# Two-layer decode attention with feed-forward: streaming K and weights past narrow operands in four column groups

## Chip, cores and metric

One core of one Trainium2 chip. The metric is the device time of the program in microseconds (us). Runs are given as a median with the lowest and highest in brackets. The ratio of two kernels is the mean time of the one's fast runs over that of the other's of the same rounds, so it is not quite the ratio of the medians quoted. The profile of a run covers one execution; its span is some 2 us shorter than the run time.

## The reference, cut to what matters

```python
# B=4 batches, 1 token each, D=512, 32 query heads, 8 K/V heads, 4096 keys, head size 128, F=1792; bf16
def A(x, k_cache, v_cache, wq, wo):
    q = (x @ wq) ...                                   # per head
    scores = einsum("bhqd,bhkd->bhqk", q, k) * Dh**-0.5
    o = einsum("bhqk,bhkd->bhqd", softmax(scores), v)
    return o.reshape(B, 1, Hq*Dh) @ wo
def Bf(x, w_gate, w_up, w_down):
    return (gelu(x @ w_gate) * (x @ w_up)) @ w_down
x = A_x
x = x + A(layernorm(x), ...);  x = x + Bf(layernorm(x), ...)
x = x + A(layernorm(x), ...);  x = x + Bf(layernorm(x), ...)   # same caches and weights again
```

Both layers read the same K and V caches. The kernel keeps the turned K of one batch on chip, so K crosses once and V twice: 114.6 MB in all. The pipeline runs over batches: attention of layer 1 for batch 0, then a **dense part** (projection, feed-forward, second-layer queries), then a **two-layer stage** (second-layer scores and softmax of batch b beside K, scores and V of the first layer of batch b+1), and so on. The dense parts of batches 1 to 3 run beside the second-layer V tiles of the batch before. A last attention and a last feed-forward over all four batches end it.

## The kernel before

K is loaded in tiles of 128x2048 bf16 (512 KB) and turned in 32x32 blocks by VectorE. A score matmul then loads 128x128 of turned K as weights and passes 16 columns of a padded query block through it. Projections and feed-forward work the same way: 128x128 of weights loaded for one column of activations.

```python
class Turner:                      # one K tile: VectorE turns it in two halves
    def step(self):
        kn = load_kv(A_k_cache, self.b, kvh, t, "k_t")          # one of 7 buffers, shared with V
        for bb in range(NB):
            nc.vector.transpose(out=self.kt[:, ..., bb], in_=kf[:, :, bb])        # 128x512 fp32

def scores_head(sc, s, kt, kvh, qb):                            # 32 pairs for a head
    for g in range(G8):
        for be in range(BE):
            nc.tensor.matmul(sc[:, s, g, :], lhsT=kt[:, g, be // 2, :, be % 2],
                             rhs=qb[:, kvh, be].rearrange("p a h -> p (a h)"), ...)

def soft_max(sc):                  # two heads at a time
    nc.vector.tensor_reduce(out=colmax[:], in_=v, axis=AX.X, op=ALU.max)
    nc.gpsimd.partition_all_reduce(gmax..., colmax..., P, RED.max)
# ... soft_exp: subtract (VectorE), exp (ScalarE); soft_sum: reduce (VectorE), all-reduce (GpSimd)

def ffn_in(b0, nb, w_sb, name):    # 56 pairs; out_proj, q_proj and down alike
    for m in range(KF):
        for k in range(KD):
            nc.tensor.matmul(h[:, m, :], lhsT=w_sb[:, k, m * P:(m + 1) * P], rhs=xn_bf[:, k, bs], ...)
```

Of the kernel before, what the change touches and what calls it, by code (L numbers as in the profile page):

```python
# [15 lines left out]
P = 128  # L16
# [3 lines left out]
CH = 16  # L20
GH = 2
QD = 4
# [3 lines left out]
KV_BUFS = 7  # L26
# [3 lines left out]
def kernel(  # L30
# [20 lines left out]
    assert Sq == 1 and Dh == P and rep == 4  # L51
# [3 lines left out]
    NT = C // CH  # L55
    NG = Hkv // GH
    G8 = C // QD
    HG = GH * rep
    assert C % CH == 0 and CH % QD == 0
# [5 lines left out]
    ktp = ctx.enter_context(tc.tile_pool(name="ktp", bufs=Hkv))  # L65
    kvin = ctx.enter_context(tc.tile_pool(name="kvin", bufs=KV_BUFS))
    qbp = ctx.enter_context(tc.tile_pool(name="qbp", bufs=2))
    rawp = ctx.enter_context(tc.tile_pool(name="rawp", bufs=2))
    p1p = ctx.enter_context(tc.tile_pool(name="p1p", bufs=2))
    p2p = ctx.enter_context(tc.tile_pool(name="p2p", bufs=NG))  # L70
    grp = ctx.enter_context(tc.tile_pool(name="grp", bufs=2))
    small = ctx.enter_context(tc.tile_pool(name="small", bufs=1))
# [3 lines left out]
    ps_acc = ctx.enter_context(tc.tile_pool(name="ps_acc", bufs=1, space=bass.MemoryType.PSUM))  # L76
    ps_misc = ctx.enter_context(tc.tile_pool(name="ps_misc", bufs=2, space=bass.MemoryType.PSUM))
# [3 lines left out]
    ident_bf = const.tile([P, P], BF16, name="ident_bf")  # L81
    make_identity(nc, ident_bf[:])
    mean_f = const.tile([P, P], FP32, name="mean_f")
    nc.vector.memset(mean_f[:], 1.0 / D)
    magic = const.tile([P, B], I32, name="magic")
    nc.vector.memset(magic[:], 0x5F3759DF)
    sel = const.tile([P, NB, 2, QD, QS], BF16, name="sel")
    for a in range(QD):
        nc.vector.tensor_copy(
            out=sel[:, :, :, a, :],  # L90
            in_=ident_bf[:].rearrange("p (b i e) -> p b e i", b=NB, e=2))
    amask = const.tile([P, QD], FP32, name="amask")
    nc.vector.tensor_reduce(out=amask[:], in_=ident_bf[:].rearrange("p (a i) -> p a i", a=QD),
                            axis=AX.X, op=ALU.max)
# [5 lines left out]
    wd_sb = wts.tile([P, KF, D], BF16, name="wd_sb")  # L100
    wq_dram = A_wq.rearrange("(k p) n -> p k n", p=P)
# [5 lines left out]
    q1_bf = state.tile([P, Hq, B], BF16, name="q1_bf")  # L107
    q2_bf = state.tile([P, Hq], BF16, name="q2_bf")
    xn_bf = state.tile([P, KD, B], BF16, name="xn_bf")

    dq = nc.sync
# [7 lines left out]


# [4 lines left out]
    def ln_center(b0, nb):  # L125
        bs = slice(b0, b0 + nb)
        st = ps_misc.tile([P, 2, nb, KD], FP32, name="st", tag="misc")
        nc.tensor.matmul(st[:], lhsT=mean_f[:, :], rhs=XX[:, :, bs], start=True, stop=True)  # L128
        mv = small.tile([P, 2, nb], FP32, name="mv", tag="mv")
        nc.vector.tensor_reduce(out=mv[:], in_=st[:], axis=AX.X, op=ALU.add)  # L130
        nc.vector.tensor_tensor(out=xn_bf[:, :, bs].rearrange("p k b -> p b k"), in0=XX[:, 0, bs],
                                in1=mv[:, 0].unsqueeze(2).broadcast_to([P, nb, KD]),
                                op=ALU.subtract)
        return mv
# [25 lines left out]
    def q_proj(b0, nb, h0, hp):  # L160
        bs = slice(b0, b0 + nb)
        qps = ps_misc.tile([P, hp, nb], FP32, name="qps", tag="misc")
        for i in range(hp):
            m = h0 + i
            for k in range(KD):
                nc.tensor.matmul(qps[:, i, :], lhsT=wq_sb[:, k, m * Dh:(m + 1) * Dh],  # L166
                                 rhs=xn_bf[:, k, bs], start=(k == 0), stop=(k == KD - 1))
        return qps

    def q_norm(qps, dst, rstd, hp, nb):  # L170
        nc.vector.tensor_tensor(out=dst, in0=qps[:], in1=spread_rstd(rstd, hp, nb), op=ALU.mult)  # L171

    def q_spread(q_rows, qb, h0, hp):
        k0, nk = h0 // rep, hp // rep
        qe = ps_misc.tile([P, nk, BE, rep], FP32, name="qe", tag="misc")
        for be in range(BE):
            nc.tensor.matmul(qe[:, :, be], lhsT=sel[:, be // 2, be % 2].rearrange("p a i -> p (a i)"),  # L177
                             rhs=q_rows, start=True, stop=True)
        nc.vector.tensor_tensor(  # L179
            out=qb[:, k0:k0 + nk].rearrange("p k n a h -> p (k n) a h"),  # L180
            in0=qe.rearrange("p k n h -> p (k n) h").unsqueeze(2)
                .broadcast_to([P, nk * BE, QD, rep]),
            in1=amask[:].unsqueeze(1).unsqueeze(3).broadcast_to([P, nk * BE, QD, rep]),
            op=ALU.mult)

    def out_proj(y, o_bf, h0, hp, first, last):
        for i in range(h0, h0 + hp):
            rhs = o_bf[:, i:i + 1] if len(o_bf.shape) == 2 else o_bf[:, i, :]
            for dk in range(KD):
                nc.tensor.matmul(y[:, :, dk], lhsT=wo_sb[:, i, dk * P:(dk + 1) * P], rhs=rhs,  # L190
                                 start=(first and i == h0 and dk == 0),
                                 stop=(last and i == h0 + hp - 1 and dk == KD - 1),
                                 skip_group_check=True)

    def add_y(b0, nb, y):
        bs = slice(b0, b0 + nb)
        nc.vector.tensor_tensor(out=XX[:, 0, bs], in0=XX[:, 0, bs], in1=y[:], op=ALU.add)  # L197

    def ffn_in(b0, nb, w_sb, name):
        bs = slice(b0, b0 + nb)  # L200
        h = ps_misc.tile([P, KF, nb], FP32, name=name, tag="misc")
        for m in range(KF):
            for k in range(KD):
                nc.tensor.matmul(h[:, m, :], lhsT=w_sb[:, k, m * P:(m + 1) * P],  # L204
                                 rhs=xn_bf[:, k, bs], start=(k == 0), stop=(k == KD - 1))
        return h

    def gelu(nb, hg, rstd):
        h = small.tile([P, KF, nb], FP32, name="h", tag="h")
        nc.vector.tensor_tensor(out=h[:], in0=hg[:], in1=spread_rstd(rstd, KF, nb), op=ALU.mult)  # L210
# [7 lines left out]
                                       in1=spread_rstd(rstd, KF, nb), op0=ALU.mult, op1=ALU.mult)  # L218
        nc.vector.scalar_tensor_tensor(out=sq[:], in0=sq[:], scalar=1.0, in1=h[:],
                                       op0=ALU.add, op1=ALU.mult)  # L220
        return sq

    def gate_up(nb, th, hu):
        H_bf = small.tile([P, KF, nb], BF16, name="H_bf", tag="H_bf")
        nc.vector.tensor_tensor(out=H_bf[:], in0=hu[:], in1=th[:], op=ALU.mult)
        return H_bf

    def down(nb, H_bf):
        y = ps_misc.tile([P, nb, KD], FP32, name="y2", tag="misc")
        for dk in range(KD):  # L230
            for k in range(KF):
                nc.tensor.matmul(y[:, :, dk], lhsT=wd_sb[:, k, dk * P:(dk + 1) * P],  # L232
                                 rhs=H_bf[:, k, :], start=(k == 0), stop=(k == KF - 1))
        return y


    KT = {}

    class Turner:
# [3 lines left out]
        def step(self):  # L243
            kvh, t = divmod(self.n, NT)
            self.n += 1
            if t == 0:
                self.kt = ktp.tile([P, G8, NB, QD, QS], FP32, name="kt", tag="kt")
                KT[kvh] = self.kt
            gt = CH // QD
            kn = load_kv(A_k_cache, self.b, kvh, t, "k_t")  # L250
            kf = kn.rearrange("p c d -> p (c d)").bitcast(FP32).rearrange(
                "p (c b i) -> p c b i", b=NB, i=QS)
            for bb in range(NB):
                nc.vector.transpose(  # L254
                    out=self.kt[:, t * gt:(t + 1) * gt, bb].rearrange("p g c j -> p g (c j)"),
                    in_=kf[:, :, bb])

    def new_scores():
        return ps_sc.tile([P, GH, G8, QD * rep], FP32, name="sc", tag="sc")

    def scores_head(sc, s, kt, kvh, qb):
        kt = kt.rearrange("p g b c j -> p (g b c j)").bitcast(BF16).rearrange(
            "p (g b m e) -> p g b m e", b=NB, m=P, e=2)
        for g in range(G8):
            for be in range(BE):
                nc.tensor.matmul(sc[:, s, g, :], lhsT=kt[:, g, be // 2, :, be % 2],  # L266
                                 rhs=qb[:, kvh, be].rearrange("p a h -> p (a h)"),
                                 start=(be == 0), stop=(be == BE - 1))

    def soft_max(sc):  # L270
        v = sc.rearrange("p s g (a h) -> p s h (g a)", h=rep)
        colmax = grp.tile([P, GH, rep], FP32, name="colmax", tag="col")
        nc.vector.tensor_reduce(out=colmax[:], in_=v, axis=AX.X, op=ALU.max)  # L273
        gmax = grp.tile([P, GH, rep], FP32, name="gmax", tag="all")
        nc.gpsimd.partition_all_reduce(gmax.rearrange("p s h -> p (s h)"),  # L275
                                       colmax.rearrange("p s h -> p (s h)"), P, RED.max)
        return gmax

    def soft_exp(sc, gmax):
# [277 lines left out]
```

## Time and profile before

| | |
|---|---|
| time | 368.95 us, median of 3 (367.92 to 370.53) |
| span of the profiled run | 373.3 us |
| traffic | 114.58 MB; a 512 KB tile takes 1.28 us at full rate |
| TensorE | 55% busy, 13,700 instructions of about 27 ns a pair |
| VectorE | 43% busy |

The profiled execution was a long one: a span of 373.3 us belongs to a run of some 375 us, 6 above the median. Its stage marks so lie up to that much late.

Two of the page's cost groups of the kernel before carry the change (columns: line, engine, operation, output and input, shapes, count, then busy us and mean ns of one, then the engine's idle time before it and what ended most of it):

```profile
L254 DVE STREAM_TRANSPOSE kt<-k_t 128x512 f32<-128x512 f32 x128 | 82.8, 686 | 26.9 <-DMA k_t<-in_A_k_cache_dram 16.8
L266 PE MATMUL sc<-qb,kt 128*128 128x16 bf16 x2048 | 63.0, 175 | 17.5 <-issue 13.6
```

The turn of K is VectorE's greatest item. The score matmuls are 2048 small ones. Their mean of 175 ns is a latency in a pipeline; the spacing is 27 ns.

### The profile page before, as it was taken

The numbers are of one execution on the slowest core, as the hardware profiler recorded it, in microseconds if no ns is written. First come the engines' busy times: TensorE is split into PE (matmuls) and PEld (weight loads), VectorE is DVE, ScalarE is ACT, GpSimd is POOL, SyncE is SP. The second block draws the span as 40 slices with busy tenths as digits, with TensorE's granted clock in tenths as the row PEclk, the third lists the DMA queues.
The fourth block names the chain that finished last, engine by engine and source line by source line (L and its number), as shares of the span: only waits on it lengthen the run. The fifth ranks groups of instructions, "written<-read, shape, count | busy, mean of one in ns | idle before, by whom it ended". The sixth has DMA issues, their size and how long they took to land.

```text
span 373.3 us, 14915 instructions
## 1 busy us (share of the span) xinstructions
PE 204.4 (55%) x6848; PEld 193.2 (52%) x6848; DVE 160.4 (43%) x502; ACT 26.5 (7%) x70; POOL 25.1 (7%) x70
## 2 busy tenths in 40 slices
PE   0435141337765545865555657656465557678645
PEld 0334141337665445764555647655465456677635
DVE  0854423303686553321777453127745523224104
ACT  0020000000011011000011010000101000001100
POOL 0000000000010111000111110000110100002000
DMA  7999999995078799999879899998888799984730
GB/s 237 421 417 383 416 375 417 395 407 228 11 253 302 234 376 363 382 313 359 288 244 386 347 329 377 358 341 275 271 332 308 265 382 413 345 311 147 248 119 2
DMA packets 36302, 115.52 MB, mean 309 GB/s; under 512 B 3208, under 2 KB 9104, under 8 KB 36240
## 3 DMA queue, kind: packets, MB, share of 16 engines
q1 hardware_dynamic: 36240, 114.58, 83.7%
q8 instruction: 53, 0.87, 0.9%
q14 instruction: 9, 0.07, 0.0%
HBM read 114.56 MB, written 0.00 MB: 307 GB/s over the span
## 4 chain that ended last, share of the span: by engine, by line
PE 38%; DMA 29%; issue 16%; DVE 15%; POOL 1%; ACT 1%; SPq 0%; ACTq 0%; POOLq 0%; DVEq 0%
DMA v_t<-in_A_v_cache_dram 29%; PE sc L266 11%; PE ot L334 10%; DVE kt L254 7%; PE qps L166 3%; PE y L190 3%; DVE colmax L273 2%; PE y L232 2%; PE hg L204 2%; PE hu L204 2%; PE x L293 1%; PE st L128 1%; DVE sc L281 1%; POOL gmax L275 1%; PE yf L190 1%
## 5 line engine op out<-in xcount | busy, mean ns | idle before, releaser
L334 PE MATMUL ot<-pe,v_t 128*128 128x4 bf16 x2048 | 68.7, 167 | 77.2 <-DMA v_t<-in_A_v_cache_dram 60.1
L334 PEld LDWEIGHTS <-v_t 128*128 128x128 bf16 x2048 | 63.7, 105 | 82.4 <-DMA v_t<-in_A_v_cache_dram 63.8
L254 DVE STREAM_TRANSPOSE kt<-k_t 128x512 f32<-128x512 f32 x128 | 82.8, 686 | 26.9 <-DMA k_t<-in_A_k_cache_dram 16.8
L266 PE MATMUL sc<-qb,kt 128*128 128x16 bf16 x2048 | 63.0, 175 | 17.5 <-issue 13.6
L266 PEld LDWEIGHTS <-kt 128*128 128x128 bf16 x2048 | 58.9, 104 | 20.0 <-issue 15.2
L273 DVE TENSOR_REDUCE colmax<-sc 128x8 f32<-128x256 f32 x32 | 13.4, 420 | 45.0 <-PE sc L266 45.0
L293 PE MATMUL x<-raw,ident_bf 128*32 128x64 bf16 x512 | 13.4, 238 | 31.1 <-ACT raw L285 28.6
L285 ACT ACTIVATE raw<-sc 128x256 bf16<-128x256 f32 x32 | 12.3, 383 | 222.6 <-DVE sc L281 222.6
L275 POOL PARTITION_ALL_REDUCE gmax<-colmax x32 | 11.9, 371 | 229.9 <-DVE colmax L273 149.7
L166 PE MATMUL qps<-xn_bf,wq_sb 128*128 128x1 bf16 (+1 forms) x640 | 20.2, 166 | 11.3 <-issue 10.1
L293 PEld LDWEIGHTS <-ident_bf 128*32 128x32 bf16 x512 | 9.8, 118 | 31.6 <-issue 30.9
L190 PEld LDWEIGHTS <-wo_sb 128*128 128x128 bf16 x640 | 19.8, 104 | 12.2 <-issue 12.2
L166 PEld LDWEIGHTS <-wq_sb 128*128 128x128 bf16 x640 | 18.9, 104 | 11.8 <-issue 11.2
L190 PE MATMUL y<-OT_bf,wo_sb 128*128 128x1 bf16 x512 | 15.8, 165 | 9.9 <-DVE OT_bf L338 6.7
L307 POOL PARTITION_ALL_REDUCE den<-cs x32 | 12.7, 398 | 85.7 <-DVE cs L304 85.7
L338 DVE TENSOR_TENSOR OT_bf<-ot,rden 128x8 bf16<-128x8 f32 (+1 forms) x23 | 3.5, 153 | 33.7 <-PE ot L334 33.7
L281 DVE TENSOR_TENSOR sc<-sc,gmax 128x256 f32<-128x256 f32 x32 | 13.5, 422 | 8.9 <-POOL gmax L275 8.7
L298 ACT CAST pe<-x 128x256 bf16<-128x256 f32 x32 | 11.9, 372 | 33.0 <-PE x L293 33.0
L304 DVE TENSOR_REDUCE cs<-raw 128x8 f32<-128x256 bf16 x32 | 12.4, 389 | 3.8 <-ACT raw L285 3.8
L171 DVE TENSOR_TENSOR q_bf<-qps,rstd 128x8 bf16<-128x8 f32 (+1 forms) x20 | 3.3, 170 | 24.0 <-PE qps L166 23.6
L197 DVE TENSOR_TENSOR XX<-XX,y 128x4 f32<-128x4 f32 (+1 forms) x9 | 1.4, 160 | 22.5 <-PE y L232 16.0
L179 DVE TENSOR_TENSOR qb<-qe,amask 128x128 bf16<-128x128 f32 (+1 forms) x23 | 7.8, 338 | 5.6 <-PE qe L177 5.5
(50 smaller groups left out, 113.2 us busy)
## 6 DMA issues: line engine op xcount, KB each, us to landing
v_t<-in_A_v_cache_dram SPq DMA_DIRECT2D x128, 512.0 KB, 7.4
k_t<-in_A_k_cache_dram SPq DMA_DIRECT2D x64, 512.0 KB, 8.8
wo_sb<-in_A_wo_dram SPq DMA_DIRECT2D x2, 2048.0 KB, 12.5
wq_sb<-in_A_wq_dram SPq DMA_DIRECT2D x2, 1024.0 KB, 9.2
wq_sb<-in_A_wq_dram SPq DMA_DIRECT2D x1, 2048.0 KB
wg_sb<-in_B_w_gate_dram SPq DMA_DIRECT2D x1, 1792.0 KB, 17.1
wu_sb<-in_B_w_up_dram SPq DMA_DIRECT2D x1, 1792.0 KB, 13.1
wd_sb<-in_B_w_down_dram SPq DMA_DIRECT2D x1, 1792.0 KB, 17.1
```

Source lines behind the costliest of these rows:

```text
L166: nc.tensor.matmul(qps[:, i, :], lhsT=wq_sb[:, k, m * Dh:(m + 1) * Dh], rhs=xn_bf[:, k, bs], start=(k == 0), stop=(k == KD - 1))
L190: nc.tensor.matmul(y[:, :, dk], lhsT=wo_sb[:, i, dk * P:(dk + 1) * P], rhs=rhs, start=(first and i == h0 and dk == 0), stop=(last and i == ...
L204: nc.tensor.matmul(h[:, m, :], lhsT=w_sb[:, k, m * P:(m + 1) * P], rhs=xn_bf[:, k, bs], start=(k == 0), stop=(k == KD - 1))
L254: nc.vector.transpose(out=self.kt[:, t * gt:(t + 1) * gt, bb].rearrange("p g c j -> p g (c j)"), in_=kf[:, :, bb])
L266: nc.tensor.matmul(sc[:, s, g, :], lhsT=kt[:, g, be // 2, :, be % 2], rhs=qb[:, kvh, be].rearrange("p a h -> p (a h)"), start=(be == 0), s ...
L273: nc.vector.tensor_reduce(out=colmax[:], in_=v, axis=AX.X, op=ALU.max)
L275: nc.gpsimd.partition_all_reduce(gmax.rearrange("p s h -> p (s h)"), colmax.rearrange("p s h -> p (s h)"), P, RED.max)
L281: nc.vector.tensor_tensor(out=w, in0=w, in1=gmax[:].unsqueeze(2).broadcast_to([P, GH, G8 * QD, rep]), op=ALU.subtract)
L293: nc.tensor.matmul(x[a * QS:(a + 1) * QS, :, :, cc, :], lhsT=ident_bf[:, cc * QS:(cc + 1) * QS], rhs=raw[:, :, :, a, :], start=True, stop= ...
L304: nc.vector.tensor_reduce(out=cs[:], in_=raw.rearrange("p s g a h -> p s h (g a)"), axis=AX.X, op=ALU.add)
L307: nc.gpsimd.partition_all_reduce(den.rearrange("p s h -> p (s h)"), cs.rearrange("p s h -> p (s h)"), P, RED.add)
L334: nc.tensor.matmul(o, lhsT=v[:, i, :], rhs=pe[:, s, c, :], start=(c == 0), stop=(c == C - 1))
```

## The change

Intent: exchange the operands. The small operand (queries, one column of activations) is loaded into 32 columns of the array, and K or the weights stream past it 512 columns at a time, four matmuls on the four column groups side by side. That is a quarter of the score instructions, and half of all of TensorE's. The results then lie as rows, which VectorE turns back in 32x32 blocks. The softmax works on four heads at once, without GpSimd. Seven K/V buffers become six, and the output-projection and feed-forward weights load after batch 0's V. Cut to its core:

```diff
-KV_BUFS = 7
+KV_BUFS = 6
+ROWS = [ps_row.tile([P, 512], FP32, name=f"rows{i}") for i in range(2)]
+def turn_rows(rows, n):
+    t = tmpp.tile([P, n // QS, QS], FP32, name="rt", tag="tmp")
+    nc.vector.transpose(out=t.rearrange("p n j -> p (n j)"), in_=rows[:, :n])
+    return t
 ...
 def ffn_in(...):                                   # out_proj, q_rows and down alike
-    for m in range(KF):
-        for k in range(KD):
-            nc.tensor.matmul(h[:, m, :], lhsT=w_sb[:, k, m * P:(m + 1) * P], rhs=xn_bf[:, k, bs], ...)
+    for k in range(KD):
+        for j in range(QD):
+            nc.tensor.matmul(rows[j * QS:j * QS + nb, :KF * QS], lhsT=xn_bf[:, k, bs], rhs=w[:, j], ...)
 ...
-        for bb in range(NB):
-            nc.vector.transpose(out=self.kt[:, ..., bb], in_=kf[:, :, bb])
+        nc.vector.transpose(out=KT[kvh][:, t * CH:(t + 1) * CH]..., in_=kn...)      # 128x1024 fp32
 ...
+def scores(sc, g, t):
+    for be in range(BE):
+        for s in range(GH):
+            ...                                # w0 picks the head's columns in QB[g], kt its turned keys
+            nc.tensor.matmul(sc[s * QS:(s + 1) * QS], lhsT=QB[g][:, w0:w0 + 2 * W],
+                             rhs=kt[:, t * CH:(t + 1) * CH, be // 2, :, be % 2], ...)
+def soft(sc):                                      # rows of 512; maximum by reduce, 32x32 turn, reduce
+    nc.vector.tensor_reduce(out=m[:], in_=sc..., axis=AX.X, op=ALU.max)
+    nc.vector.transpose(out=mt[:], in_=m[:].broadcast_to([P, QS]))
+    ...
+    nc.scalar.activation(out=pp[:, 0], in_=sc[:], func=ACT.Exp, bias=nm[:, 0:1], scale=scale, accum_out=ls[:])
 ...
 def attend(b2, b1, rstd1):                         # two-layer stage, in VectorE's order
+    for g in range(NG):
+        for t in range(NT): scores(sc2[g], g, t)   # second layer, batch b2
+    p0 = soft(sc2[0]); turn(2); ... ; p0 = soft(sc2[1]); build_q1(b1, 0); turn(2); ... ; build_q1(b1, 1)
+    scores(sc1, 0, 0); turn(4); scores(sc1, 0, 1)  # first layer, batch b1
+    turn(2); p0 = soft(sc1); turn(1); ... ; turn(1)
+    for i in range(4):
+        vals.step(); turn(1)                       # the first V tile comes after 12 K turns
```

## The prediction

> **What bounds the kernel now.** I read the page's chain of waits first, then busy tenths and DMA rate, then windows cut at the stage borders, and last the chain in order of time for one batch.
>
> ```profile
> PE 38%; DMA 29%; issue 16%; DVE 15%; POOL 1%; ACT 1%; SPq 0%; ACTq 0%; POOLq 0%; DVEq 0%
> ...
> q1 hardware_dynamic: 36240, 114.58, 83.7%
> q8 instruction: 53, 0.87, 0.9%
> ```
>
> No engine is full: PE is busy 55% and DVE 43% of the span, yet PE holds 38% of the chain, transfers 29%, and "issue" (PE without anything the profile shows it waiting for) 16%. The floor is the traffic: 114.6 MB, which neither version changes. The windows (columns: busy time of PE, PEld, DVE, ACT, POOL, then clock, DMA share, GB/s) show where the stream breaks:
>
> ```profile
> 24.00:82.00 58.00, 18.07 (x595) 16.89 (x594) 19.64 (x44) 2.27 (x6) 2.29 (x6) 1.00 1.04 400
> 82.20:99.00 16.80, 13.94 (x453) 13.35 (x451) 6.78 (x42) 0.21 (x1) 0.00 (x0) 1.00 0.43 173
> 99.00:153.40 54.40, 31.88 (x1085) 29.97 (x1084) 31.42 (x77) 6.04 (x16) 6.11 (x16) 1.00 0.84 293
> 229.00:253.40 24.40, 16.38 (x568) 16.09 (x568) 6.57 (x39) 0.21 (x1) 0.00 (x0) 1.00 0.96 349
> 253.40:310.00 56.60, 32.00 (x1081) 29.98 (x1078) 31.95 (x80) 6.04 (x16) 6.10 (x16) 1.00 0.86 308
> 332.50:361.00 28.50, 19.13 (x650) 17.78 (x651) 5.96 (x19) 2.92 (x8) 3.03 (x8) 1.00 0.57 197
> ```
>
> The first attention pass (24 to 82) runs at full DMA rate. The dense part of batch 0 (82 to 99) drops to 173 GB/s: nothing to consume, so after seven prefetched tiles the queue stands. The two-layer attention stages (99 to 153, 253 to 310) get about 300 GB/s, the last one 197. A 512 KB tile at the full 410 GB/s (my reading of one-microsecond windows with a full queue) takes 1.28 us. A batch in steady state moves 48 tiles, 61.4 us at that rate, but takes 75.6 and 81.3 us (last V tile used at 153.3, 228.9 and 310.2).
>
> The "issue" pieces, start and length, in one dense part:
>
> ```profile
> 232.82 3.07 issue
> 235.89 0.24 PE ot L334 x3
> 236.14 1.49 PE hu L204 x56
> 237.63 0.85 PE ot L334 x32
> 238.48 0.98 PE y L232 x37
> 239.47 0.43 issue
> ```
>
> Between the two stalls lie 3+56+32+37 = 128 weight-load/matmul pairs, 256 instructions; 128 pairs again lie between the stalls at 243.8 and 249.3. That is a refill period: 53 instruction packets carry 0.87 MB, 16 KB each. At 27 ns a pair PE eats 16 KB in 3.4 us, faster than a refill lands in a full DMA queue.
>
> **What the Trainium skill says.** "Runtime: NRT & Kernel Launch", Terms: instruction memory is refilled in 16 KiB blocks. The 128-pair spacing agrees. "TensorE: Matmul & The Clock Gate", Measured speedup vs the span model: three 32-column groups with N=512 ran 2.38 times as fast as one after another. The trace before has a small case: the 16 swap matmuls of 64 columns, on four column groups, hold PE 0.33 us before the next kind starts (258.07 to 258.40), 20.6 ns each, below the 26.7 ns that 64 columns need alone at the page's 2.4 GHz. So groups overlap, by how much at N=512 no run before shows. "TensorEngine Tiling (Array Packing)", Feature Incompatibilities: column tiling excludes fast weight load. The change loads at most 32 columns, so I charge nothing. "VectorE: DVE Perf Modes", Why PSUM operands drop a tier: fp32 from PSUM runs at 1x. The fp32 turn of 512 elements from SBUF already costs 0.605 us (pairs of 1.21 us in the chain), about one element a cycle, so I charge the same from PSUM.
>
> **The change part by part.**
>
> PE. The instruction order shows PE going from 13,668 rows to 6,818. Scores go from 2048 pairs of about 27 ns (55 us) to 512 matmuls of N=512. If four overlap perfectly each costs 213/4 = 53 ns; scaled by the page's 2.38 of 3 it is 67 ns: an estimate of 34 us in all, 4.3 us for a batch's 64. Projections (160 + 160 matmuls) and feed-forward (230) cost about as much as their 2560 narrow pairs did scaled: 37 against 59 us (the page's groups, 19.8+20.2+20 us). PV stays at 2048 pairs, 55 us. Halving the instructions and slowing each streaming one gives some 700 instructions per 20 us dense part instead of about 1100, so I expect refill stalls to shrink from 58 us of chain to under 15, mostly beside transfers.
>
> DVE. K turns: 128 of 0.605 us become 64 of 128x1024, about 1.14 us (saves some 4 us). Softmax: 32 times (0.42+0.42+0.39) us = 39 us, with two POOL reductions each, becomes 16 times (max over 512, 0.69 by 0.42+256/0.96 GHz; three small ops 0.2 each; turn of bf16 0.6; one small 0.2) = 33 us. New: 30 row turns of 0.6 us = 18 us. In sum DVE is about as busy as before, 150 to 160 us.
>
> Dense part alone (no fill). Before, 82.2 to 99.0: 16.7 us. After: wo 32 matmuls about 2 us instead of 3.4, ffn 3 x 1.0 instead of 3 x 1.6, q 1.9 instead of about 4, so 5 us saved; but six turns of 0.6 and two row selections of 0.5 us are added in series, with 2 us of semaphores and small ops. The chain comes to 17.5 us: no gain in itself. What matters is what lies beside it. In batch 0 the new order loads wo and the three feed-forward weights after the V tiles, so 5.5 MB (13.4 us) load during the dense chain where the queue stood before.
>
> Walk through the stages (us from the start). DMA starts at 2.7; K, V and wq and wo end at 68 (with 2.3 us lost where the second wq piece waits for the first projection), wg 72, wu 77, wd 81. From wd the chain needs 9 us: scores of the next batch start at 90 (before: 99).
> Attention with two layers: in the new order 12 K tiles come first, paced by DVE: scores half 2.1, statistics 1.3, two turns 2.3, soft turn 0.8, statistics 1.3, q build 0.9, two turns, soft turn and build 1.8, six turns 6.8 and so on: the 12th turn ends 24 us after the start, the 16th at about 31. Six buffers cover 7.7 us, so the queue stands briefly twice; from there V is transfer-bound and the last of 32 tiles lands at 46 (ideal 41; before 54 to 57).
> Dense parts of batches 1 to 3: 16 V tiles are spread along a chain of about 20 us, 16 x 1.28 = 20.5: transfer-bound (before 22.5 to 24.4, with 8 us of refill stalls).
> So the last V tile of batch 1 lands at 136 (before 153), then +66.7 twice: 203 (229), 269 (310). Dense part 3 to 290. The last attention: 16 tiles plus a microsecond of stall, 311.5 (361). Tail: the final dense chain of 4 columns, 15 us with out-projection (before 12.4): 326.6 against 373.3. The profiled run is 4.4 us longer than the median, so 322; I add 4 us for waits that a walk misses. **326 us**.
>
> **The rivals.** (1) The groups don't overlap with N=512 (a stride-2 bf16 stream in each). Then 64 scores cost 13.6 us instead of 4.3, two passes a batch, plus 10 us in q and feed-forward: some 25 us a batch, about 400 us. Against it: 20.6 ns for 64 columns, and the page's 2.38. I give it 6%. A half case, 100 ns a matmul, gives 340. (2) DVE becomes the bound: K turns, statistics and row turns are in one in-order queue, and POOL's share of the softmax has moved there. K stage of 31 us instead of the 24 us that its transfers need is in my walk; if turns from PSUM or the dependent small ops cost 30% more, 5 us a batch, 340 to 345. For it: before, DVE was 58% busy in the two-layer stages. (3) Transfers bind everywhere, and DVE and refills hide wholly: 2.7 + 114.6 MB/410 GB/s (279) + 9 + tail 15 = 306, less 4: 302. Against it: six buffers instead of seven.
>
> **Range and chances.** Between (3) and a half case of (1) or (2): 308 to 348 should hold it 8 in 10. A gain over 2% fails only if groups hardly overlap or DVE is far slower than by sizes: faster 0.90, same 0.05, slower 0.05.
>
> **What would show it.** Scores at 53 to 75 ns each by their spacing: overlap right; near 213: rival (1). "Issue" under 5% of the chain: refills were instruction-bound. DMA at 390 GB/s or more in dense parts of batches 1 to 3, and near 350 in two-layer stages, with the queue waiting for DVE's K turns there: the walk is right. DVE over 80% busy in those stages and the queue standing: rival (2). DMA not standing between 82 and 90: the moved weights paid. A turn of rows from PSUM far over 0.65 us would make the dense chain longer than its 16 tiles and the prediction too low.

## The result and the profile after

The changed kernel took **379.14 us** (377.60 to 381.42, 4 runs), the kernel before in the same rounds 369.74 us (367.92 to 373.40). The ratio is 1.0325, 95% interval 1.0234 to 1.0416: slower by 3%, where I had said 326 us. The result is correct, and all runs count as fast.

From the page of the kernel after, the lines that answer to those of before, chain, queues and cost groups:

```profile
DMA 33%; DVE 30%; PE 27%; SPq 4%; issue 3%; ACT 1%; ACTq 0%
...
q1 hardware_dynamic: 35744, 114.58, 84.0%
q8 instruction: 27, 0.44, 0.5%
...
L317 DVE STREAM_TRANSPOSE kt<-k_t 128x1024 f32<-128x1024 f32 x64 | 75.8, 1219 | 14.8 <-DMA k_t<-in_A_k_cache_dram 14.6
L331 PE MATMUL sc<-kt,qb 128*32 128x512 bf16 x512 | 62.4, 580 | 12.6 <-DVE kt L317 11.5
L198 DVE STREAM_TRANSPOSE rt<-rows 128x512 f32<-128x512 f32 (+1 forms) x30 | 20.8, 692 | 39.1 <-PE rows L257 16.9
```

The part of the mechanism that I counted on happened: instruction packets fell from 53 to 27, and "issue" from 16% to 3% of the chain. But the time did not follow. VectorE doubled its share of the chain, 15% to 30%, and transfers rose from 29% to 33%. It looks as if the refill stalls had been lying beside other waits, and those now end last; no run isolates the stalls.

Windows of the kernel after, cut at the stage borders (columns as in the prediction: start and end, length, busy us of PE, PEld, DVE, ACT, POOL, then clock, DMA share, GB/s):

```profile
155.20:180.60 25.40, 20.36 (x388) 12.61 (x388) 11.59 (x51) 0.21 (x1) 0.00 (x0) 0.57 0.94 329
180.60:232.40 51.80, 30.85 (x465) 15.12 (x462) 28.50 (x54) 5.45 (x12) 0.00 (x0) 0.53 0.91 327
...
180.60:206.10 25.50, 13.96 (x152) 5.01 (x150) 20.76 (x38) 4.09 (x9) 0.00 (x0) 0.57 0.82 283
206.10:232.40 26.30, 16.89 (x313) 10.11 (x312) 7.74 (x16) 1.36 (x3) 0.00 (x0) 0.50 0.99 371
```

A dense part (155.2 to 180.6) reaches 329 GB/s where I had promised a full stream. The two-layer stage splits into two halves: first 25.5 us in which VectorE is busy 20.8 us (81%) and the queue moves 283 GB/s, then 26.3 us at 371 GB/s. The chain in order of time of that first half (start, length, what; dots for pieces left out):

```profile
180.66 3.56 PE sc L331 x29
...
184.24 0.70 DVE m L337
...
185.63 2.28 DVE kt L317 x2
187.91 0.59 DVE pp L355
...
190.41 0.42 DVE qb L232
190.83 2.28 DVE kt L317 x2
193.11 0.60 DVE pp L355
...
195.00 6.78 DVE kt L317 x6
201.78 0.59 DVE m L337
```

From 184.2 on it is one in-order VectorE queue: statistics of the second layer, two turns, statistics, two turns, then six. Only at 206 have twelve K tiles been turned. The single operations cost what I had written (1.14 us a turn, 0.6 to 0.7 the rest). The half of the scores does not: 32 matmuls take 3.56 us, 111 ns each, against the 67 of my sum. (Such a piece includes the tail of its last matmul; from start to start they are 106.7 ns apart.)

The queue's own waits say what held the transfers up (SyncE issues them; columns: us in total, times, longest), first in 180.60 to 206.10, then in 206.10 to 232.40:

```profile
SPq L115 <- DVE kt L317: 19.9, 12, 5.1
...
SPq L115 <- PE ot L395: 11.6, 11, 3.1
```

In the first half a load waits until VectorE has turned a K tile and so freed its buffer; VectorE itself waited only 1.1 us for K in the whole stage. In the second half a load mostly waits until TensorE has used a V tile.

**Where the 50 us of error lie.** I cut the traces at two marks: the start of the second layer's scores, and the start of the last output-projection burst, which follows the last V tile by less than a microsecond. Mean of the three stages of a kind; the last column is the one experiment that changes three things at once (e16_all, below). The columns add up to the span (in the prediction, to its 326.6).

| us | predicted | after | e5 half streams | e2 half turns | e6 both | e7 buffers | e16 all |
|---|---|---|---|---|---|---|---|
| start to the first two-layer scores | 90 | 103.3 | 100.6 | 103.8 | 98.6 | 94.0 | 90.2 |
| two-layer stage, 3 times | 46 | 52.7 | 50.8 | 48.2 | 45.6 | 47.8 | 41.0 |
| dense part, 3 times | 20.7 | 24.2 | 22.8 | 24.3 | 22.6 | 23.5 | 21.0 |
| last attention | 21.5 | 28.9 | 25.3 | 27.6 | 25.9 | 22.1 | 21.7 |
| rest | 15 | 14.2 | 13.8 | 15.1 | 13.8 | 15.1 | 13.7 |

So the error is 13.3 us in the first stage, 3 x 6.7 = 20 in the two-layer stages, 3 x 3.5 = 10.5 in the dense parts and 7.4 in the last attention. Against the kernel before, the walk is nearly level: first scores at 103.3 (before 99.0), last V tile of batch 3 at 308.8 (310.2), last attention's at 360.6 (361), and the tail after it costs 16.5 instead of 12.4. Since the profile of before is that of a run 6 us above its median, these marks don't show where the 9 us between the medians were lost.

### The profile page after: what moved, and what is told of

Its sections match the earlier page's. It is cut to its first block, busy times and chain, and to the rows that moved or that the text cites. A ratio compares the mean times of both kernels' runs of the same rounds, so it can differ in the third digit from the quotient of the medians.

```text
span 377.1 us, 8073 instructions
## 1 busy us (share of the span) xinstructions
PE 216.9 (58%) x3522; PEld 114.9 (30%) x3522; DVE 175.4 (47%) x476; ACT 24.2 (6%) x54; POOL 0.7 (0%) x6
## 4 chain that ended last, share of the span: by engine, by line
DMA 33%; DVE 30%; PE 27%; SPq 4%; issue 3%; ACT 1%; ACTq 0%
DMA v_t<-in_A_v_cache_dram 21%; DVE kt L317 13%; PE ot L395 7%; DMA k_t<-in_A_k_cache_dram 7%; PE sc L331 7%; DMA wd_sb<-in_B_w_down_dram 5%; DVE rt L198 3%; PE rows L208 3%; SPq L125 3%; PE rows L301 2%; DVE pp L355 2%; PE rows L257 2%; DVE m L337 2%; PE ot L388 2%; PE st L157 1%
## 5 line engine op out<-in xcount | busy, mean ns | idle before, releaser
L317 DVE STREAM_TRANSPOSE kt<-k_t 128x1024 f32<-128x1024 f32 x64 | 75.8, 1219 | 14.8 <-DMA k_t<-in_A_k_cache_dram 14.6
L331 PE MATMUL sc<-kt,qb 128*32 128x512 bf16 x512 | 62.4, 580 | 12.6 <-DVE kt L317 11.5
L198 DVE STREAM_TRANSPOSE rt<-rows 128x512 f32<-128x512 f32 (+1 forms) x30 | 20.8, 692 | 39.1 <-PE rows L257 16.9
L331 PEld LDWEIGHTS <-qb 128*32 128x32 bf16 x512 | 18.4, 126 | 44.7 <-issue 41.4
L257 PE MATMUL rows<-wo_sb,OT_bf 128*1 128x512 bf16 (+1 forms) x160 | 20.5, 609 | 9.5 <-DMA wo_sb<-in_A_wo_dram 8.5
L350 ACT ACTIVATE pp<-sc,nm 128x512 bf16<-128x512 f32 x16 | 11.0, 687 | 170.7 <-DVE junk L346 156.8
L337 DVE TENSOR_REDUCE m<-sc 128x1 f32<-128x512 f32 x16 | 10.8, 678 | 20.8 <-PE sc L331 20.7
L208 PE MATMUL rows<-wq_sb,xn_bf 128*1 128x512 bf16 (+1 forms) x160 | 17.5, 605 | 1.0 <-DVE msq L167 1.0
L355 DVE STREAM_TRANSPOSE pp<-pp 128x512 bf16<-128x512 bf16 x16 | 11.0, 687 | 6.6 <-ACT pp L350 6.6
L157 PEld LDWEIGHTS st<-XX,mean_f 128*128 128x128 f32 x20 | 5.0, 312 | 25.1 <-issue 21.7
L388 PE MATMUL ot<-zx,mean_f 128*128 128x16 f32 x32 | 9.5, 376 | 0.0
```

Source lines behind the costliest of these rows:

```text
L198: nc.vector.transpose(out=t.rearrange("p n j -> p (n j)"), in_=rows[:, :n])
L208: nc.tensor.matmul(rows[j * QS:j * QS + nb, :], lhsT=xn_bf[:, k, bs], rhs=w, start=(k == 0), stop=(k == KD - 1))
L257: nc.tensor.matmul(rows[r0:r0 + nb, :], lhsT=lhsT, rhs=wo_sb[:, i, :], start=(i < QD), stop=(i >= Hq - QD))
L317: nc.vector.transpose(out=KT[kvh][:, t * CH:(t + 1) * CH].rearrange("p c b j -> p (c b j)"), in_=kn.rearrange("p c d -> p (c d)").bitcast( ...
L331: nc.tensor.matmul(sc[s * QS:(s + 1) * QS], lhsT=QB[g][:, w0:w0 + 2 * W], rhs=kt[:, t * CH:(t + 1) * CH, be // 2, :, be % 2], start=(t == ...
L337: nc.vector.tensor_reduce(out=m[:], in_=sc.rearrange("p c j -> p (c j)"), axis=AX.X, op=ALU.max)
```

## The experiments

The theory after the result: three things on the path that my walk had wrong or left out. TensorE's clock is half of what I took; VectorE's in-order queue holds up the release of K/V buffers; and with six buffers no transfer runs ahead to make up for it. The rivals were that only one of them counts, or that something else (the queue, the order, the width of the feed-forward) does.

### The clock: e1_warm, e4_probe, e5_halfstream

e1_warm puts unused matmuls with N=512 into TensorE's waits, to raise the granted clock:

```diff
+    def warm(n):
+        w = ps_x.tile([P, 512], FP32, name="wm", tag="x")
+        for _ in range(n):
+            nc.tensor.matmul(w[:], lhsT=wq_sb[:, 0, :P], rhs=wq_sb[:, 0, :512], start=True, stop=True, ...)
+    ... warm(2) at each V tile, warm(3) to warm(9) at waits for VectorE
```

> The changed kernel plus about 400 unused full-array matmuls of N=512 into a spare PSUM bank, placed where TensorE otherwise waits (two after every V tile, three to nine at the waits of the K stage). Theory A (the half clock is the main cause): granted clock goes from 0.60 to over 0.9, the 32 score matmuls of a half fall from 3.56 us to 1.7-2.1 us, the 32 q matmuls from 3.56 to about 1.9, dense parts of batches 1 to 3 from 25 to 21-22 us, and the time from 379 to 350-362. Theory B (VectorE's in-order queue paces the K stage and the transfers starve behind six buffers): clock rises just as far but the time stays within 372-380, because the first and last K turn of a two-layer stage stand 20 us apart either way.

Measured: 397.28 us (391.27 to 401.09; two of four runs slow; the fast ones 391.27 and 394.34), ratio 1.0668 (1.0567 to 1.0770). The mean clock rose from 0.60 to 0.79, and 32 scores took 1.97 us, 62 ns each with the tail, 55 from start to start. But the unused matmuls took 16% of the chain themselves. What a faster clock is worth **this run can't tell**; what a matmul costs at full and at half clock it does.

e4_probe is the kernel before with four 128-column matmuls of N=512 for each group of heads:

```diff
+                w = ps_x.tile([P, 512], FP32, name="wm", tag="x")
+                for _ in range(4):
+                    nc.tensor.matmul(w[:], lhsT=ident_bf[:], rhs=qb1..., start=True, stop=True, ...)
```

> The kernel before, with four unused full-array matmuls of N=512 after the first-layer scores of each head group. Their spacing tells what the printed clock of 1.00 in its profile means: 213 ns each if TensorE really ran at full clock, 427 ns if it was at half clock all along and no event had been recorded. I expect 427 ns, because the changed kernel's first 48 matmuls of N=512, while its page still prints 1.00, are 106 to 119 ns apart in four column groups, as they are later at a printed 0.50. Time within 2% of before.

Measured: 374.68 us (one run, its state unknown). A clock of 1.00 is printed for it, as for before, and yet all 48 recorded probes, from 19.9 to 304.0 us, last 587 to 634 ns and start 0.43 us apart, twice the 0.22 us of the unused matmuls of the same size in e1_warm where they last 380 ns. So the kernel before ran at half clock, as far as the probes reach; its narrow pairs (27 ns) don't show it.

e5_halfstream leaves out half of all streamed matmuls (wrong on purpose):

```diff
-        for be in range(BE):
+        for be in (0, 1):                     # scores; projections and feed-forward: half of the k loop
```

> Wrong result on purpose: of every group of streamed matmuls (scores, q, gate, up, down, out-projection) only half is issued, so at the half clock (111 ns each) they cost what the prediction had charged for all of them (67 ns each, or 53 at best). Nothing is put on the path, other than in the run with unused matmuls. Theory A (clock): the score half falls from 3.56 to 1.8 us, dense parts from 24.8 to about 21 us, the first turn comes 1.7 us earlier; 379 falls to 355-363. Theory B (VectorE paces the K stage): 370-377, because the 25 us K stage keeps its VectorE work.

Measured: 364.55 us (362.27 to 365.58), ratio 0.9882 (0.9814 to 0.9950), 15 us under the kernel after. The result is wrong, as meant. The time lies just above what theory A had said (355 to 363) and under B's. The gain lies in all stages (table). It is the worth of half of the streams, not of the clock: 97% of e5's score matmuls last over 550 ns, against 81% in the kernel after, so the clock was if anything lower.

The tile queries (duration in ns, lowest, median and highest, then first and last start) of the scores of e1_warm and of the kernel after, of the probes, and of the scores of e6_halfboth, followed by a window of the latter:

```profile
L338 PE MATMUL sc<-kt,qb x64: 376/389/413, 108.8 to 112.2; 128*32 128x512 bf16 x64
...
L331 PE MATMUL sc<-kt,qb x64: 383/628/628, 180.6 to 186.4; 128*32 128x512 bf16 x64
...
L419 PE MATMUL wm<-qb,ident_bf x12: 587/634/634, 108.7 to 145.5; 128*128 128x512 bf16 x12
...
L333 PE MATMUL sc<-kt,qb x32: 608/628/632, 98.6 to 101.6; 128*32 128x512 bf16 x32
...
166.88:185.10 18.22, 10.03 (x104) 3.40 (x102) 14.61 (x38) 3.91 (x9) 0.00 (x0) 1.00 0.95 345
```

A streaming matmul lasts 376 to 413 ns at full clock and some 628 at half. The kernel after is at 628 for most of a stage. The last two lines belong together: in e6_halfboth all 256 score matmuls last 582 to 632 ns while the window prints a clock of 1.00. That 1.00 is an absence of records, not a clock (such a page has no PEclk row), and the same 1.00 in the profile of before was what I had built on. The mean clocks mislead likewise: in the profile of the kernel after the records begin at 32 us, and what lies before counts as 1.00, though its score matmuls from 29.2 us on last 607 to 609 ns.

### VectorE's turns: e2_halfturn, e6_halfboth

e2_halfturn turns only half of each K tile (zeros in the rest; wrong on purpose, though the comparison passed it):

```diff
-                    out=KT[kvh][:, t * CH:(t + 1) * CH]..., in_=kn...)
+                    out=KT[kvh][:, t * CH:t * CH + CH // 2]..., in_=kn[:, :CH // 2]...)
```

> Wrong result on purpose: every K turn does only half of its tile (the other half of the turned keys is zero), so VectorE has 0.6 us less work at each of 64 K tiles; loads and matmuls stay. Theory A (clock): the two-layer stages shorten by under 2 us each and the time stays at 372-379. Theory B (VectorE paces the K stage): the K stage loses up to 12 x 0.58 = 7 us in each of three two-layer stages, the DMA rate in them rises from about 310 to 350 GB/s or more, and the time falls to 356-364.

Measured: 367.44 us (363.29 to 369.58), 12 us under the kernel after by the medians; two of the four runs count as slow, so no ratio is given, and the two fast ones are 15 us under. The median lies between what the two theories had said, the fast runs at the upper end of B's. Nearly all of the gain lies where K is turned, the two-layer stages (52.7 to 48.2), and nothing in the dense parts (24.2, 24.3). My walk had priced the turns rightly: this shows that they lie on the path, not that their cost was mistaken.

e6_halfboth is e2 and e5 together (wrong on purpose).

> Wrong result on purpose: half of the streamed matmuls and half of each K turn. If the two costs lie one after the other on the path (K turns wait for scores, scores for the dense part), their gains add: the half turns alone gave about 12 us, so 345-352. If removing one merely uncovers the other or the transfers, 360-366. What stays above the predicted 326 is then neither clock nor VectorE, but the first 100 us and the transfers.

Measured: 347.44 us (344.60 to 347.85), ratio 0.9432 (0.9368 to 0.9497), 32 us under the kernel after. That is about the sum of the two alone (12 to 15, and 15): they add, as far as the noise lets one tell.

### The buffers: e7_buffers, e8_hold, e9_inplace

e7_buffers has ten K/V buffers in place of six. To make room, the up weights are not loaded and only half of down's are, 2.75 MB or 6.7 us of transfers at 410 GB/s less (wrong on purpose).

```diff
-KV_BUFS = 6
+KV_BUFS = 10
-    wu_sb = wts.tile([P, KD, F], BF16, name="wu_sb")
+    wu_sb = wg_sb
```

> Wrong result on purpose: the up weights are not loaded (gate's are used twice) and only half of the down weights, 2.75 MB less (6.7 us less transfer at most, in the first 100 us), and the freed memory makes ten K/V buffers of six. If transfers starve because six buffers are handed back in ones and twos by VectorE, the two-layer stages (51.8 us each) fall to 46-48 us, and the time to 355-362. If the K stage is paced by VectorE's work alone, only the loads' 7 us and a little more go: 368-374, with two-layer stages of 50-52 us.

Measured: 346.93 us (344.15 to 350.01; one of four slow), ratio 0.9387 (0.9312 to 0.9462), 32 us under the kernel after, 25 without the weights' 6.7. That is more than expected (355 to 362), with the stage where it was expected: 47.8, and the last attention falls to 22.1, though no engine has less to do. TensorE's clock can have helped only a little: 64 scores took 5.5 us, not 6.2. The first half of a stage stays as it was (twelfth turn at 25.1 us, 303 GB/s). The queue's waits in the second half (188.80 to 212.10) say where the gain lies: for TensorE's V matmuls 3.1 us instead of 11.6, otherwise for the transfers themselves:

```profile
SPq L115 <- DMA v_t<-in_A_v_cache_dram: 9.0, 9, 1.5
SPq L115 <- PE ot L394: 3.1, 1, 3.1
```

e8_hold keeps six of the sixteen second-layer V tiles back for the K half of the next stage, where the queue stands (right result): `fill(3)` and `fill(2)` to `fill(1)` in the dense part, `held(1)` in six places of the stage.

> An attempt at a better kernel: of the 16 V tiles of the previous batch's second layer that the dense part consumes, six are held back and consumed in the K stage, where TensorE waits for VectorE and the DMA rate is only 283 GB/s; all results stay right. If the dense part (24.8 us, more than 16 tiles of 1.28 us) is bound by its chain and the K stage has room in TensorE and DMA, dense parts shrink by 2.5 to 3 us, two-layer stages grow by 0 to 1, in two of the three batches with a previous one: 370-376. If the held tiles delay the scores or the turns, no gain: 378-383.

Measured: 383.64 us (382.26 to 384.95), ratio 1.0408 (1.0342 to 1.0473): 4.5 us worse. The tiles held occupy buffers, and the turns of K now wait for their loads, 26.5 us in 16 waits (14.6 in 8 after).

e9_inplace loads K into the place where its turned form will stand, so that K needs no buffer, and loads six V tiles ahead (right result):

```diff
-                kn = load_kv(A_k_cache, self.b, kvh, t, "k_t")
-                nc.vector.transpose(out=KT[kvh][...], in_=kn...)
+                nc.vector.transpose(out=kt, in_=kt)      # the load went straight to kt
+            vals.preload(6)
```

> A candidate that keeps all of the change but loads each K tile straight into its place among the turned keys and turns it there, so that K tiles take no K/V buffer: all 16 K loads of a batch are released by the end of the second-layer scores, six V tiles are loaded ahead of them, and the q weights are in two tiles. All results stay right. VectorE's work and TensorE's clock are as in the changed kernel. If the starved queue (six buffers handed back in ones and twos) is the largest cause, as the run with ten buffers says, the two-layer stages fall from 51.8 us to 40-44, the first 100 us lose 5 to 8, and the time is 335-348. If VectorE's order of work paces the stage, it stays above 48 us and the time is 365-375.

Measured: 379.97 us (377.13 to 382.51), ratio 1.0279 (1.0220 to 1.0338): no gain, where I had expected 335 to 348. K's loads now come all at once: VectorE waits 25.1 us in 7 waits for K. Then the queue stands, at 70 GB/s or less from 204 to 212, until the first V tile is used. I then took the order to be at fault, and e13 tested it.

### Smaller rivals: e3_wqsplit, e10_inplace_lite, e11_narrowffn, e12_inplace_narrow

e3_wqsplit gives the two halves of the q weights a tile each, so that the first projection waits for its half alone.

> The q weights in two tiles instead of one, so that the load of the second half does not wait until the first projection has read the first half; all else is the same. If the stand of the DMA queue at 23.4 to 28.1 us comes from that wait, the stand is gone, the weights end 4 to 5 us earlier and the time is 374-375. If the queue would have stood anyway (buffers held by VectorE), nothing changes, 378-379.

Measured: 382.31 us (379.10 to 383.16), ratio 1.0367 (1.0294 to 1.0440). No gain, though the stand at 23.4 to 28.1 us is gone (418 GB/s): the queue all but stands from 41 to 46 instead, and the first two-layer scores start at 104.1 instead of 103.3.

e10_inplace_lite is e9 with about 30 unused matmuls a batch, at waits only.

> The candidate with some 30 unused matmuls of N=512 a batch, only where TensorE waits for VectorE in the K stage and one after each V tile of the first layer. If these hold TensorE at full clock into the dense part and the next scores, at no cost in the path, 8 to 12 us less than the candidate without. If the clock falls again in the dense part, or the unused matmuls lie in the path, no gain, 0 to +8.

Measured: 380.55 us (379.42 to 382.96), ratio 1.0311 (1.0255 to 1.0367). As e9.

e11_narrowffn takes gate, up and down back to narrow pairs and so their row turns away:

```diff
-        hg = turn_rows(rows, KF * QS)[:, :, :nb]
+        hg = rows                              # pairs with 128x128 weights again, as before
```

> The changed kernel with one part undone: gate, up and down again load the weights and stream one column (168 pairs of 27 ns, 4.5 us a dense part) instead of 46 streamed matmuls at 111 ns (5.1 us) with three turns of rows by VectorE and one selection. By the page's rows the three turns (0.65, 0.65, 0.73) and the selection (0.3) lie in the dense chain: about 2.3 us less in each of five dense parts, but instruction refills come back. If the turned rows cost what they show, 379 becomes 368-373; if refills or transfers bind instead, 377-381.

Measured: 375.12 us (371.66 to 377.90; two of six slow), ratio 1.0113 (1.0047 to 1.0180): 4 us under the kernel after by the medians, 6 by the fast runs, most of it after the last attention (12.9 us to the end instead of 14.2) and in the first stage (102.1). A refill stall is back in a dense part, 2.44 us at 163.2. So streaming the feed-forward was a small loss.

e12_inplace_narrow is e9 and e11 together.

> The candidate with the narrow feed-forward of the run before. If the dense chain still binds its 16 V tiles there, 4 to 10 us less than the candidate; if the dense part is then bound by transfers, only the tail and batch 0 gain: 2 to 4 us.

Measured: 372.69 us (372.30 to 376.59), ratio 1.0114 (1.0057 to 1.0171), 7 us under e9 and level with e11.

### The order: e13_order, e14_order_narrow, e15_order_inplace

e13_order has the kernel after's work in another order: the first layer's queries and eight K turns first, the second layer's softmaxes behind the first V tiles (right result).

```diff
-            p0 = soft(sc2[0]); turn(2); ...; p0 = soft(sc2[1]); build_q1(b1, 0); turn(2); ...
+            build_q1(b1, 0)
+            turn(4); scores(sc1, 0, 0); turn(4); scores(sc1, 0, 1)
+            turn(1); p0 = soft(sc1); turn(1); ...
+            for i in range(6):
+                vals.step(); turn(1)          # second-layer softmaxes at i = 0 and i = 3
```

> The changed kernel with its own work in another order in the attention stage: the first layer's q block and its K turns come first, the second layer's two softmaxes move behind the first V tiles, so that the first V tile is used some 18 us after the scores begin and no longer 26 to 30. Right result. If VectorE's order starves the transfers (my theory now): two-layer stages 45 to 47 us in place of 51.8, total 355 to 365 us. If the six buffers or the turns bind by themselves: stages stay at 51 to 53 us and the total at 375 to 382.

Measured: 375.41 us (372.11 to 376.83), ratio 1.0203 (1.0117 to 1.0288). 4 us less than the kernel after, with intervals that overlap, where I had expected 14 to 24. **My theory of the order fell**, and the windows of e13_order say why:

```profile
180.87:206.00 25.13, 13.55 (x173) 5.82 (x171) 20.13 (x33) 2.19 (x6) 0.00 (x0) 0.70 0.98 351
206.00:231.84 25.84, 16.14 (x314) 9.47 (x311) 9.05 (x23) 3.27 (x7) 0.00 (x0) 0.50 0.91 315
```

The first half of the stage now moves 351 GB/s instead of 283, and the second 315 instead of 371. In the second half the queue now waits 15.0 us in 12 waits for TensorE's V matmuls (11.6 in the kernel after), and 8.25 us of the chain are one K load; the turns end no later (the sixteenth 35.5 us after the start, before 36.0). The order shifts the loss within a stage (52.7 to 50.4 us) but doesn't remove it, and the first two-layer scores start 4.3 us later (107.6).

e14_order_narrow is e13 with e11's narrow feed-forward.

> The same order, with gate, up and down projections narrow again as in the kernel before (no row turns there). If the row turns bind in the feed-forward once the order is mended: 4 to 6 us less than e13_order, 350 to 360 us. If not: within 2 us of it, or more because the TensorE refills come back.

Measured: 370.36 us (368.66 to 372.00), ratio 1.0085 (1.0007 to 1.0164). It is 5 us under e13, as expected, and 10 above the 350 to 360 forecast.

e15_order_inplace is e12 with an order near e13's: no buffers for K, an early first V tile, but only the second of the second-layer softmaxes moves behind the V tiles.

> K loaded and turned in place, six V tiles ahead, narrow feed-forward (all as in e12), and the order of e13: the first layer's K turns ahead of the second layer's second softmax, so that the first V tile is used some 25 us after the scores begin, when the K transfers just end. Right result. If buffers and order hide each other: two-layer stages of 45 to 47 us, no stretch of a standing queue in them, 350 to 360 us in all. If each was worth only what it gave alone: 365 to 372 us. If neither matters and the clock and the dense chain bind: 370 to 375.

Measured: 371.20 us (368.31 to 373.65), ratio 1.0024 (0.9972 to 1.0077). No better than e14; its two-layer stages stay at 52 us on the mean (49.8, 53.5, 52.7). So in this combination buffers for K and order do not hide each other. Of the right kernels e15 comes level with the kernel before, e14 within 2% of it, and none beats it.

### All three at once: e16_all

e6 and e7 together (wrong on purpose): half the turns, half the streams, ten buffers, 2.75 MB less (2.6 in the text on record was rounded wrongly).

> Wrong result on purpose. Half of the K turns and half of the streamed matmuls (as e6), and ten K/V buffers with 2.6 MB less of weights (as e7), all at once. If these three terms are the whole miss: 315 to 328 us, the two-layer stages at 41 to 44 us and near 400 GB/s. If a further cause stands behind them (a chain of dependent small operations, the queue itself): 333 to 345 us, little under e6 and e7 alone (347 each).

Measured: 313.38 us (312.98 to 314.37), ratio 0.8513 (0.8431 to 0.8595), 66 us under the kernel after, of which 6.7 are the weights left out. A two-layer stage and the dense part before it, windows of e16_all:

```profile
130.60:151.50 20.90, 15.46 (x328) 10.71 (x326) 11.45 (x51) 0.22 (x1) 0.00 (x0) 0.50 1.03 408
151.50:192.00 40.50, 24.38 (x407) 13.33 (x404) 20.23 (x54) 5.45 (x12) 0.00 (x0) 0.50 1.03 408
```

Both move 408 GB/s: the queue never stands, and a batch takes 61.4 us, exactly the 48 tiles of 1.28 us that I had called its transfers. The clock is still half (0.50), so a full clock is not needed for that, only less work per clock. In the steady batches nothing further stands behind the three terms. Two limits: halving the turns and the streams takes away more than my walk had wrong (a stage of 41.0 is under my 46), so this doesn't split the miss among the three; and the first stage takes 90.2 us with 6.7 us less to load, where I had 90 with all of it.

## Why the prediction was wrong, point by point

- **Refill stalls shrink from 58 us of chain to under 15: right** (16% to 3% of the chain), but "mostly beside transfers" was where it ended: no gain followed the 47 us taken from "issue". I had taken the share of a chain for time that can be had. It was time in which no other reason was named for TensorE's wait; VectorE's queue and the transfers took its place in the chain.
- **The groups overlap: right; 67 ns a matmul: wrong.** Four groups of N=512 start 106.7 ns apart at half clock, a quarter of a probe's 427, and 55 at full: the overlap is all but complete. "If four overlap perfectly each costs 213/4 = 53 ns" is right at a clock that was seldom there: the profile of before printed 1.00 because it held no clock record. The cost is that of the half case (100 ns) that I gave 340 us, but by the clock and not by half an overlap. Halving the streams (e5) is worth 15 us, together with the turns 32. (A slip in the sum: the 2560 narrow pairs are 2120, 640 + 640 + 840; the 59 us beside them, from the page, stand.)
- **VectorE as busy as before, 150 to 160 us: nearly right** (175). A turn of 128x1024 took 1.13 to 1.16 us in the chain and 1.22 on the mean (1.14 predicted), a row turn 0.69 on the mean (0.6).
- **Two-layer stage of 46 us: the step that failed most.** I wrote that "six buffers cover 7.7 us, so the queue stands briefly twice; from there V is transfer-bound and the last of 32 tiles lands at 46". The twelfth turn ended at 25.5 us, and I had said 24: VectorE's pace was nearly right, the overlap of the transfers with it was not. In these 25.5 us the queue waited 19.9 us for K turns to free buffers and moved 283 GB/s, 13.8 tiles' worth where e16's 408 GB/s make 19.8. That is 7.8 us lost, not a brief stand. And from there V was not transfer-bound: the queue waited 11.6 us for TensorE's V matmuls to free buffers, and 371 GB/s for 26.3 us lose another 2.4. Together this is nearly all by which the 51.8 us to the last V tile exceed the ideal 41. Fewer turns (e2: 48.2) and more buffers (e7: 47.8) each mend part of it. The same assumption lay in the last attention, "16 tiles plus a microsecond of stall": 28.9 instead of 21.5, and 22.1 with ten buffers. And my range, 308 to 348, rested on it too.
- **Dense parts transfer-bound at 20.5 us: wrong**, 24.2 and 329 GB/s. The chain there is longer than the transfers: with ten buffers the queue is full (406 GB/s in e7, 140.1 to 163.7) and the part still takes 23.5. The streams at half clock are a good part of it (q takes 3.3 to 3.6 us where I had 1.9, gate 1.66 where I had 1.0): e5 takes 22.8, e16, with half of the streams and ten buffers, 21.0.
- **"DMA not standing between 82 and 90": right, and of no use.** The moved weights do load there, at 373 GB/s from 68.0 to 93.4, but the last of them lands at 93.4, not 81: the queue had stood from 23.4 to 28.1 and from 43.5 to 46.0, and the rate is below 410. The first two-layer scores so start 13 us late. e3 removed the first of these stalls and gained nothing; with ten buffers and fewer weights they start at 94.0, of which up to 6.7 us are the loads left out. What the rest of the 13 us is stays open.
- **Rival (2), VectorE, was half right**: in the K half it is 81% busy with the queue waiting, but over the whole stage 55% (28.5 of 51.8 us), and not because its operations cost 30% more. Its price, 340 to 345, was too low because the half clock and the buffers came on top: turns, streams and buffers changed alone gave 12 to 15, 15 and 25 us, together 59 without the weights.

What stays open: how much of e5's 15 us a warm clock alone would give. The unused matmuls that raised it cost more than they gave, and the mean clocks printed for the four runs of the kernel after (0.60, 0.62, 0.70, 0.70 with 378.9, 379.4, 381.4 and 377.6 us) can't be used: in the kept profiles of other runs some 0.60 goes with clock records that begin at 32 us, some 0.70 with records that begin at 92 to 106 us. Which part of the change makes it slower than the kernel before is shown in part only: the narrow feed-forward gives back 4 to 6 of the 9 us (e11). And no right kernel here has ten buffers, so their 25 us are not on offer.

## What to carry to other kernels

A few buffers don't make transfers overlap with a slow consumer for a whole stage: once they are taken, each load waits for the consumer to free one. Look at the waits of the queue that issues the loads before calling a stage transfer-bound; here they were 19.9 us on VectorE and then 11.6 us on TensorE. A share of the chain of waits is no saving until the next waits behind it, here VectorE's queue and the transfers, have been shown to be shorter. Before replacing many narrow matmuls by long streams, put one long matmul into the old kernel as a probe: a clock printed as 1.00 may only mean that nothing was recorded.

## What the Trainium skill lacked or had wrong

- "TensorE: Matmul & The Clock Gate", Seeing it yourself, HAM trace caveats (HAM is the page's name for what sets the clock): it warns that clock events in a trace can be unreliable. It does not say that the trace of a kernel full of matmuls may hold none at all, which reads as full clock: e6_halfboth prints 1.00 for the whole run while its score matmuls last 582 to 632 ns, against 376 to 413 at full clock (e1_warm), and the kernel before did the same (probes 587 to 634 ns).
- The same page, Measured speedup vs the span model: it has 2.38 times for three groups at N=512. Here a stream of four groups overlapped all but fully: 106.7 ns from start to start at half clock, where probes on the whole array start every 427 ns, and 55 ns at full clock, where they start every 217.
- No page has what filling TensorE's waits to keep its clock up costs in a kernel bound elsewhere: with 334 recorded matmuls of N=512 more, the mean clock went from 0.60 to 0.79 and the time from 379 to 391 and 394 us in the two fast runs.
